# Half-head products for a second batch and an earlier 144 KB load, in a kernel whose instruction order is fixed by a scheduler

## The chip, the cores and the metric

The kernel runs on one core of a Trainium2 chip. The metric is device time in microseconds (us). "Clock" is the mean TensorE clock granted in an execution, 1.0 being full speed. Ratios are the mean time of one kernel's fast runs over the mean of the other's fast runs of the same rounds, so they are not quite the ratio of the medians quoted beside them. Square brackets after a ratio hold its 95% interval. Core engines: TensorE (PE; its weight loads are PEld), VectorE (DVE), ScalarE (ACT), GpSimd (POOL), and SyncE (SP), which issues the loads.

## The reference

Linear attention, then a ResMLP block, for 8 batches, 8 heads, 576 positions, 64 columns per head, in fp32:

```python
kv  = np.einsum('bhsd,bhse->bhde', k, v)
out = np.einsum('bhsd,bhde->bhse', q, kv)
rms = np.sqrt(np.mean(out * out, axis=-1, keepdims=True) + 1e-06)
x   = out / rms * g_norm                       # then heads side by side: (8, 576, 512)
a1  = alpha1 * x + beta1
u   = x + lam * np.einsum('ts,bsd->btd', w_tok, a1)
a2  = alpha2 * u + beta2
y   = u + lam * (np.maximum(a2 @ w_ch1, 0.0) @ w_ch2)     # 512 -> 2048 -> 512
```

The weights are shared by all batches. Until some 48 us the core's DMA engines are nearly always busy with q, k, v and the weights (in the kernel before a mean share of 0.95 from 0 to 48 us, at 341 GB/s); after that TensorE is the bound (busy 312.23 of the 316 us from 48 to 364).

## The kernel before

The Python program records every operation with an engine, a cost estimate in us, its reads and its writes. A list scheduler then fixes the order of each engine **at build time**, from those estimates. At run time an engine works through its list and waits where data is missing, even if the next entry is ready: in the trace of the kernel before, TensorE stands still for 1.14 us, to 41.38 us, for `wst4`, with k'v of batch 1 behind it in the list, whose v had landed at 31.96 us.

q·kv of the first two batches (`R32 = 2`) is done in fp32r. A chunk pair is 256 positions; the fifth chunk (the tail) has 64:

```python
def f32(e):
    if nc_ > 1:                                  # a pair of chunks
        for h in range(nh):
            w = qtr[:, h0 + h, 2 * cs[0]:2 * cs[0] + 2, :].rearrange("p k s -> p (k s)")
            for x in range(1 if nh < 8 else 2):  # 8 heads: two matmuls of N=64 per head
                y = slice(0, 128) if nh < 8 else slice(64 * x, 64 * x + 64)
                # ... o: where the result goes
                mm = e.matmul(o, w, kvr[:, h0 + h, y], start=True, stop=True)
    else:                                        # the tail: 128 rows, 64 of them zeros
        for h in range(h0, hs.stop):
            p = 64 * (h // 4)
            mm = e.matmul(t.flat()[:, 64 * (h - h0):64 * (h - h0) + 64],
                          qtrt[:, h % 4, :], kvr[:, h, p:p + 64], start=True, stop=True)
    return mm
if b < R32:
    P.op("PE", 0.058 * m, f32, cold=True, # ... its reads and writes
```

```python
for hs in (HALVES if b == 0 else ALL):           # batch 0 by half the heads, batch 1 all at once
    for cs in ((0, 2), (1, 3), (4,)):
        yield lambda cs=cs, hs=hs: group(cs, hs)
```

The order of the loads, and the load of the last 64 rows of w_tok into `wst4` ("t2"). "w0" to "w3" are the slices of w_ch1, "w4" and later those of w_ch2, "Bk", "Bv", "Bq" are k, v and q of batch 1:

```python
order = ["k0", "v0", "q0", "k1", "t0", "v1", "q1", "t1",
         "w0", "g", "w1", "w2", "Bk", "Bv", "w3", "Bq", "lam", "a2", "t2", "w4",
         "w5", "w6", "w7"]
# ...
P.op("SP", 0.6, lambda e: e.dma_start(wst4[:], moe_w_tok[8:576:9, :]),
     w=[("wst", 4)], dma_us=0.9, at=sp["t2"])
```

## Time and profile before

| | kernel before |
|---|---|
| device time, median of 3 runs | 365.87 us (364.91 to 366.12) |
| span of the profiled execution, clock | 364.2 us, 0.993 |
| TensorE busy | 357.3 us, 98% |
| TensorE idle for `wst4` at 41.38 us | 1.14 us |
| start of the first channel product (L954) | 32.23 us |
| k'v of batch 1 (L602), at half clock | 3.18 us for 140 matmuls |
| channel product 1 of batch 0 done | 59.89 us |
| start of the last addition | 360.28 us |

The last rows are milestones of TensorE's list, read from the chain that ended last. The lines themselves are in the prediction below.

### The profile page before, as it was taken

How to read it: one execution, taken by the hardware profiler on the slowest of the kernel's cores; microseconds unless marked ns; L12 is line 12 of the kernel's file. 1: busy time of each engine (PE TensorE's matmuls, PEld its weight loads, DVE VectorE, ACT ScalarE, POOL GpSimd, SP SyncE). 2: the span in 40 equal slices, each digit the busy share in tenths (PEclk: the TensorE clock that was granted, in tenths of full speed). 3: DMA queues.
4: the chain of work that ended last, by engine and by line, in shares of the span. 5: the costliest groups of instructions: out<-in, count | busy, mean ns of one | idle time of the engine just before them, and what ended most of it. 6: DMA issues, size and time to landing. Idle time of an engine off the chain costs nothing.

```text
span 364.2 us, 8018 instructions
## 1 busy us (share of the span) xinstructions
PE 357.3 (98%) x3594; PEld 215.2 (59%) x3354; DVE 211.4 (58%) x310; ACT 143.7 (39%) x252; POOL 116.2 (32%) x93
## 2 busy tenths in 40 slices
PE   8999899999999999999999999999999999999995
PEld 6888685466754554457654554457754554457644
DVE  3557699872686189823885189724884288620021
ACT  2675057127750158107730157007730156007500
POOL 4377185910064005700281015800751005300000
PEclk9999899999999999999999999999999999999999
DMA  7999996028865677667816684586836510340023
GB/s 286 355 384 363 323 350 250 0 49 113 237 249 117 115 202 283 104 125 170 314 32 127 117 277 174 108 123 142 337 66 124 117 29 2 72 96 21 2 58 86
DMA packets 67558, 59.17 MB, mean 162 GB/s; under 512 B 45552, under 2 KB 45828, under 8 KB 67524
## 3 DMA queue, kind: packets, MB, share of 16 engines
q1 hardware_dynamic: 67472, 58.66, 58.4%
q8 instruction: 27, 0.44, 0.5%
q14 instruction: 7, 0.06, 0.0%
q10 hardware_dynamic: 52, 0.01, 0.0%
HBM read 38.60 MB, written 9.44 MB: 132 GB/s over the span
## 4 chain that ended last, share of the span: by engine, by line
PE 91%; DMA 5%; SPq 2%; ACT 1%; issue 0%; DVE 0%
PE ps L988 34%; PE ps L938 19%; PE ps L923 13%; PE ps L787 8%; PE ps L602 5%; DMA wst<-in_moe_w_tok_dram 3%; DMA vf<-in_v_dram 3%; PE ps L397 2%; PE ps L682 2%; PE ps L1146 2%; PE ps L800 1%; PE ps L695 1%; PE ps L570 1%; SPq L506 1%; PE ps L1189 0%; SPq L1106 0%
## 5 line engine op out<-in xcount | busy, mean ns | idle before, releaser
L988 PE MATMUL ps<-w,ht 128*128 128x512 bf16 (+1 forms) x592 | 129.0, 373 | 0.0
L988 PEld LDWEIGHTS ps<-w,ht 128*128 128x128 bf16 x592 | 56.8, 98 | 64.1 <-issue 1.6
L912 ACT ACTIVATE ht<-ps,bias 128x640 bf16<-128x640 f32 (+2 forms) x98 | 72.5, 742 | 46.4 <-PE ps L938 38.7
L938 PE MATMUL ps<-a2t,w 128*128 128x320 bf16 x512 | 71.9, 299 | 0.0
L762 POOL TENSOR_TENSOR xm<-xm,g_bc 128x1024 f32<-128x1024 f32 (+1 forms) x16 | 33.4, 2085 | 114.9 <-DVE rt L759 112.4
L938 PEld LDWEIGHTS ps<-a2t,w 128*128 128x128 bf16 x512 | 49.5, 98 | 20.3 <-DVE xm L755 0.3
L923 PE MATMUL ps<-a2t,w 128*128 128x512 bf16 x240 | 54.6, 379 | 0.0
L999 DVE TENSOR_TENSOR xm<-ps,xm 128x512 f32<-128x512 f32 (+1 forms) x33 | 22.1, 673 | 53.4 <-PE ps L988 53.4
L633 ACT ACTIVATE kvd<-ps 64x256 bf16<-64x256 f32 x24 | 9.1, 378 | 99.8 <-PE ps L602 99.6
L733 DVE TENSOR_REDUCE small<-sq 128x16 f32<-128x1024 f32 (+3 forms) x27 | 24.8, 928 | 22.9 <-ACT sq L731 22.7
L923 PEld LDWEIGHTS ps<-a2t,w 128*128 128x128 bf16 x240 | 22.7, 98 | 25.1
L787 PE MATMUL ps<-rt,wt 128*128 128x512 bf16 x140 | 31.4, 379 | 0.0
L913 DVE TENSOR_SCALAR ht<-ps,bias 128x512 bf16<-128x512 f32 (+2 forms) x34 | 24.8, 738 | 10.3 <-PE ps L923 4.7
L534 POOL TENSOR_TENSOR qs<-qf,qs 128x512 bf16<-128x512 f32 x14 | 18.5, 1319 | 25.8 <-ACT qs L493 24.8
L731 ACT ACTIVATE sq<-ps 128x1024 f32<-128x1024 f32 (+3 forms) x27 | 21.3, 799 | 12.9 <-PE ps L397 8.2
L771 DVE TENSOR_TENSOR xm<-ps,xm 128x512 f32<-128x512 f32 x28 | 19.1, 688 | 8.9 <-PE ps L787 8.6
L787 PEld LDWEIGHTS ps<-rt,wt 128*128 128x128 bf16 x140 | 13.7, 98 | 16.5
L999 DVE TENSOR_TENSOR xtl<-ps,xtl 128x512 f32<-128x512 f32 x4 | 2.8, 692 | 35.5 <-PE ps L988 35.5
L602 PEld LDWEIGHTS ps<-vf,kf 64*64 64x64 f32 x1152 | 18.9, 140 | 3.5 <-issue 2.5
L602 PE MATMUL ps<-vf,kf 64*64 64x64 f32 x1152 | 20.1, 227 | 0.4 <-DMA vf<-in_v_dram 0.2
L755 DVE TENSOR_TENSOR xm<-ps,small 128x1024 f32<-128x1024 f32 (+1 forms) x18 | 19.7, 1100 | 0.2
L759 POOL TENSOR_TENSOR rt<-xm,e_bc 128x512 bf16<-128x512 f32 (+1 forms) x6 | 9.8, 1635 | 28.4 <-DVE xm L755 27.4
(105 smaller groups left out, 349.5 us busy)
## 6 DMA issues: line engine op xcount, KB each, us to landing
stg<-in_moe_w_ch_dram SPq DMA_DIRECT2D x8, 1024.0 KB, 12.5
kf<-in_k_dram SPq DMA_DIRECT2D x7, 1152.0 KB, 6.6
vf<-in_v_dram SPq DMA_DIRECT2D x7, 1152.0 KB, 8.7
qf<-in_q_dram SPq DMA_DIRECT2D x7, 1152.0 KB, 10.2
out_dram<-xm SPq DMA_DIRECT2D x62, 128.0 KB, 2.4
kf<-in_k_dram SPq DMA_DIRECT2D x2, 576.0 KB, 5.7
vf<-in_v_dram SPq DMA_DIRECT2D x2, 576.0 KB, 9.4
qf<-in_q_dram SPq DMA_DIRECT2D x2, 576.0 KB, 8.3
```

Of the source, the lines that this page charges most:

```text
L602: m = e.matmul(t.ap(slice(64 * i, 64 * i + 64))[:, y, 64 * x_:64 * x_ + 64], kf[rows, x, c], vf[rows, x, c], start=(c == 0), stop=(c == 8) ...
L731: P.op("ACT", act_us(64 * m), lambda e: e.activation(both(sqv), raw(), ACT.Square), r=[t], w=[("sq", sqs)])
L733: P.op("DVE", dve_us(64 * m), lambda e: e.tensor_reduce(out=smv, in_=sqv, axis=AX.X, op=ALU.add), r=[("sq", sqs)], w=[("sm", sms)], pri=-20)
L755: P.op("DVE", dve_us(64 * m), lambda e: e.tensor_tensor(out=x3, in0=raw(), in1=inv(), op=ALU.mult), r=[t, ("sm", sms)], w=xk, pri=-200)
L762: P.op(dve_pool(64 * m) if b < 2 else "POOL", pool_us(64 * m), lambda e: e.tensor_tensor(out=x3, in0=x3, in1=gb, op=ALU.mult), r=xk + ["g" ...
L787: m = e.matmul(t.flat(), wt[:, sc if sc < 4 else 4 + b % 2, 128 * c:128 * c + 128], rt[:, rs(b, sc), :], start=(sc == 0), stop=(sc == 4))
L912: return e.activation(dst, src(), ACT.Relu, bias=bi)
L913: return e.tensor_scalar(out=dst, in0=src(), scalar1=bi, scalar2=0.0, op0=ALU.add, op1=ALU.max)
L923: m = e.matmul(t.flat(), w1[:, dj, 128 * fj:128 * fj + 128], a2t[:, dj, 0:512], start=(dj == 0), stop=(dj == 3))
L938: m = e.matmul(t.ap()[:, i, 0:320], w1[:, dj, 128 * fj:128 * fj + 128], a2t[:, dj, 320 * i:320 * i + 320], start=(dj == 0), stop=(dj == 3))
L988: m = e.matmul(t.flat()[:, 0:m_], ht[:, fj, 128 * c:128 * c + 128], w2[:, fj, lo:hi], start=(fj == 0), stop=(fj == 15))
L999: P.op("DVE", dve_us(m_), lambda e: e.tensor_tensor(out=x, in0=t.flat()[:, 0:m_], in1=x, op=ALU.add), r=[t] + keys, w=keys)
```

## The change

Its intent: give batch 1 the cheaper form of q·kv that batch 0 already has, and bring in the last w_tok rows before they are needed.

```diff
-                            for x in range(1 if nh < 8 else 2):
-                                y = slice(0, 128) if nh < 8 else slice(64 * x, 64 * x + 64)
-                                o = (t.flat().rearrange("p (c h d) -> p c h d", c=2, d=64)[
-                                    :, :, h, :] if nh < 8 else t.cols(64 * (nh * x + h), 64))
-                                mm = e.matmul(o, w, kvr[:, h0 + h, y], start=True, stop=True)
+                            o = t.flat().rearrange("p (c h d) -> p c h d", c=2, d=64)
+                            mm = e.matmul(o[:, :, h, :], w, kvr[:, h0 + h, :],
+                                          start=True, stop=True)
                     else:
                         for h in range(h0, hs.stop):
-                            p = 64 * (h // 4)
+                            r_ = slice(64 * (h // 4), 64 * (h // 4) + 64)
                             mm = e.matmul(t.flat()[:, 64 * (h - h0):64 * (h - h0) + 64],
-                                          qtrt[:, h % 4, :], kvr[:, h, p:p + 64],
+                                          qtrt[r_, h % 4, :], kvr[r_, h, r_],
...
-                    P.op("PE", 0.058 * m, f32, cold=True,
+                    P.op("PE", 0.1 + (0.06 if nc_ > 1 else 0.12) * m, f32, cold=True,
...
-            for hs in (HALVES if b == 0 else ALL):
+            for hs in (HALVES if b < R32 else ALL):
...
-                 "w0", "g", "w1", "w2", "Bk", "Bv", "w3", "Bq", "lam", "a2", "t2", "w4",
+                 "w0", "g", "w1", "w2", "Bk", "Bv", "t2", "w3", "Bq", "lam", "a2", "w4",
...
-             w=[("wst", 4)], dma_us=0.9, at=sp["t2"])
+             w=[("wst", 4)], slack=4.0, dma_us=0.9, at=sp["t2"])
```

The tail's 64 rows belong to the halves: with 128 rows and halves in batch 1, the race analysis finds that half 0's tail reads rows which half 1's copy still writes. Lines after the cuts shift by two or three (L695 is L692 in the changed kernel, L699 is L697, L1146 is L1144, L923 is L921, L988 is L986, L954 is L952).

## The prediction

> **What bounds the kernel now.** I read the page first, then the chain that ended last in order of time, then one-microsecond windows around the only gap, then the groups of the lines that the change touches. The page's busy times come first, to see which engine could be the bound:
>
> ```profile
> PE 357.3 (98%) x3594; PEld 215.2 (59%) x3354; DVE 211.4 (58%) x310; ACT 143.7 (39%) x252; POOL 116.2 (32%) x93
> PE 91%; DMA 5%; SPq 2%; ACT 1%; issue 0%; DVE 0%
> ```
>
> The first line is busy time: TensorE 98%, everything else under 60%. The second is the chain by engine: TensorE carries 91% of the span. So a microsecond of TensorE work counts in full, if it lies where the chain runs over TensorE. That has to be looked up in the chain in order of time (start, length, what):
>
> ```profile
> 31.09 10.16 DMA wst<-in_moe_w_tok_dram
> 41.25 0.14 issue
> 41.38 1.24 PE ps L1146 x16
> ...
> 42.82 3.13 PE ps L602 x138
> ...
> 50.38 3.49 PE ps L695 x32
> ...
> 54.75 0.81 PE ps L699 x8
> ...
> 360.28 0.42 DVE xm L999
> ```
>
> From 41.38 to 360.26 us every piece is TensorE. Ahead of it stands a transfer: the last 64 rows of w_tok (the tile wst4, "wst" in the profile), issued at 31.09 us as the last of five and landed at 41.25 us. TensorE's timeline shows the gap that it makes:
>
> ```profile
> 39.30 0.94 PE L1215 MATMUL ps<-b2hl,w 128*128 128x2 bf16 x32
> 41.38 1.24 PE L1146 MATMUL ps<-ident,wst 64*64 64x64 f32 x16 [1.14 <-DMA wst<-in_moe_w_tok_dram]
> ```
>
> TensorE stands still for 1.14 us, though other work (the k'v of batch 1, slices 2 and 3 of the first channel product) had its data; the order is fixed at build time and has the transposes first. The windows show a second price. Columns after the times are busy PE, PEld, DVE, ACT and POOL, then granted clock, DMA share and GB/s:
>
> ```profile
> 40.00:41.00 1.00, 0.24 (x10) 0.15 (x7) 0.45 (x3) 0.00 (x0) 0.00 (x0) 1.00 1.02 252
> 41.00:42.00 1.00, 0.62 (x10) 0.65 (x12) 0.00 (x0) 0.00 (x0) 0.00 (x0) 0.79 1.10 401
> 42.00:43.00 1.00, 1.00 (x32) 1.00 (x33) 0.14 (x1) 0.34 (x1) 0.00 (x0) 0.50 1.00 371
> 43.00:44.00 1.00, 1.00 (x50) 1.00 (x47) 0.61 (x3) 0.04 (x1) 0.27 (x1) 0.50 1.04 381
> 44.00:45.00 1.00, 1.00 (x49) 1.00 (x45) 1.00 (x2) 0.00 (x0) 1.00 (x1) 0.51 1.04 385
> ```
>
> Right after the gap the granted clock is 0.50 for over 3 us. The whole change therefore acts between some 28 and 56 us, and its effect is read there.
>
> [...] the trace's fp32r q.kv with 64 moving columns runs at 3.49/32 = 109 ns each[...]. [...] w_ch1's last slice, q of batch 1, lam and alpha2 were issued before wst4, and it landed 10.16 us after its issue though it has 144 KB. [...] Here a square of 128x512 takes 597 ns and one of 128x1024 1024 ns, so a split costs 170 ns.
>
> **The change part by part.**
>
> (1) q.kv of batch 1 by head halves. Removed: 32 matmuls with 64 moving columns, 3.49 us in the chain. Added: 16 with 128 columns, one weight load per head and chunk pair in place of two. Batch 0 already does it so: in the same chain "17.64 1.04 PE ps L695 x8", 0.130 us each. 16 x 0.130 = 2.08 us; saved 3.49 - 2.08 = **1.41 us**, all on the path.
>
> (2) The tail chunk (both fp32r batches) contracts over the 64 rows that hold data instead of 128 zero-padded ones. Same count, same 128 weight columns[...]. Now 8 take 0.81 us together and 4 alone 0.56 us; in batch 1 eight become two groups of four, which may cost up to 2 x 0.56 - 0.81 = 0.31 us. I take **+0.1 us**.
>
> (3) Vector work of batch 1, whose six groups replace three. VectorE: reduce 4 x 0.681 - 2 x 1.213 = +0.30, normalise 4 x 0.690 - 2 x 1.224 = +0.31, tails 2 x 0.406 - 0.684 and 2 x 0.416 - 0.695 = +0.27, reciprocals 4 x 0.168 + 2 x 0.165 - 2 x 0.241 - 0.199 = +0.32: 1.2 us. ScalarE: squares 4 x 0.597 - 2 x 1.024 = +0.34, tail 2 x 0.377 - 0.592 = +0.16, three more square roots at 0.29 = +0.88: 1.4 us. It lies beside TensorE work. VectorE is busy 15.26 of 16.20 us from 48 to 64.2, so this is not free for it; but the finer groups start earlier, and the next thing that needs them has room: batch 1's last rt product ends at 62.66 and its token product starts at 64.21; its last transposed chunk is copied at 78.5 and the channel product that reads it starts at 82.81. I count **0**, with a risk below.
>
> (4) wst4 issued before w_ch1's last slice, whose issue waits for a buffer until 28.32 us. It can then go out right after v of batch 1, at about 18.3 us, 13 us earlier. The queue moves some 380 GB/s in these windows, so 144 KB delay what follows by 0.4 us: w_ch1's last slice lands near 35.1 instead of 34.7, while its channel products run after 47 us. From lam and alpha2 on the sum of bytes is the same. wst4 should land before 30 us, over 9 us ahead of need. Saved: the gap, **1.14 us**.
>
> (5) With the gap gone the clock should stay up. Price of the slow window: k'v of batch 1, 3.18 us for 140 matmuls, against 2.26 us for 144 in every later batch (15.7 ns each, 2.20 us): 0.98. Transposes: 16 in 1.24 us (78 ns) against 64 in 4.37 us (68 ns) for the earlier rows: 0.15. Together **1.1 us**.
>
> (6) slack=4.0 and the new cost estimates only alter the order that the list scheduler fixes. They add no operations; they shuffle the order from about 10 us on. I take **+0.3 us** for it.
>
> Sum if all comes off: 1.41 - 0.1 + 1.14 + 1.1 - 0.3 = 3.25 us. Weighing the clock part at 0.85 leaves 3.1 us: 365.87 - 3.1 = **362.8 us**, 0.8% less.
>
> **The rivals.** (a) The gap moves: TensorE runs into another transfer. DMA engines are above 0.8 share nearly everywhere to 48 us, and TensorE will be some 2 us early at k'v. For it: q of batch 1 and the w_ch2 slices land late (w_ch2's first at 43.7). Against it: [...] w_ch2 is first needed at 59.7. A new wait would give back up to 1 us: near 364. (b) The clock still drops[...]. Against it: from 16.4 to 22 us TensorE runs fp32 transposes almost alone at clock 1.00, and k'v of batch 2 at full rate. [...] That makes 363.9. (c) VectorE and GpSimd become the bound between 50 and 83 us: three w_ch2 products run on GpSimd only at 65.12 to 69.95 and are needed at about 76.8, and TensorE arrives 3 us earlier, with up to 2 us of added vector work. Slack of about 5 us speaks against a stall, but it shrinks. If it bites, 1 to 2 us are lost: 364 to 365. (d) Better than the sum: the new order also removes filler matmuls before 32 us. There TensorE follows the loads, so I expect little: 361.5 at best.
>
> **Range and chances.** The floor of the change is part (1) alone, about 364.5; all parts with a lucky order give 361.3. I take 361.3 to 364.8. A gain over 2% would need 7.3 us, more than twice all parts; a loss over 2% would need a new stall of 10 us in a stretch that has slack. So 0.02 faster, 0.97 same, 0.01 slower.
>
> **What the changed profile would show.** (1) q.kv in batch 1 as 16 matmuls 128x128 at about 0.130 us. (2) Tail matmuls on 64 rows, 0.10 to 0.14 us apart. (4) wst4 issued near 18 us, no TensorE gap on it, its transposes anywhere from 32 us on. (5) Clock 1.00 throughout 32 to 56 us and k'v of batch 1 in about 2.3 us. (3) No TensorE idle between 50 and 83 us. Wrong would be: a TensorE gap with another releaser, a clock of 0.5 in another window, or the start of the first channel product (32.23 us now) moved by more than 0.5 us.

The sum came to 1.41 - 0.1 + 1.14 + 1.1 - 0.3 = 3.25 us, or 3.1 with the clock part at 0.85. Three steps are estimates: that the clock stays up once the gap is gone, for which the trace shows only that half clock began at 41.57 us, 0.19 us after the gap ended; that the tails cost 0.1 us, within the 0 to 0.31 us named; and, in rival (a), that q of batch 1 arrives in time.

## The result, and the profile after

| kernel, set of runs | median us (lowest to highest) | ratio to the kernel before |
|---|---|---|
| changed, first set, 4 executions | 363.75 (363.61 to 364.51) | 0.9956 [0.9932, 0.998] |
| changed again, second set, 5 | 363.37 (363.17 to 363.76) | 0.9928 [0.9914, 0.9941] |
| changed again, third set, 5 | 363.12 (363.0 to 363.56) | 0.9935 [0.992, 0.9951] |
| before, in the same three sets, 4 / 11 / 11 | 365.51 / 366.02 / 365.75 | |

The gain is 0.4% to 0.7%, so within 2%. The first time lies 0.95 us above the predicted 362.8 and inside the range. That could pass for a confirmation; the trace says otherwise. First the page of the changed kernel: busy times, and the chain by engine.

```profile
PE 353.6 (98%) x3543; PEld 213.6 (59%) x3335; DVE 207.1 (57%) x321; ACT 147.5 (41%) x262; POOL 113.1 (31%) x93
PE 93%; DMA 3%; DVE 1%; SPq 1%; issue 1%
```

TensorE's share is unchanged. In the chain DMA fell from 5% to 3%, which is the `wst4` load that left it. The chain in order of time (start, length, what), the changed kernel:

```profile
34.03 3.51 PE ps L952 x32
...
41.37 1.12 PE ps L1144 x16
...
43.20 2.26 PE ps L602 x144
...
55.07 3.40 PE ps L921 x15
58.47 7.34 PE ps L986 x34
...
358.60 0.42 DVE xm L997
```

TensorE's timeline (start, length with the modelled tail, what; a wait in brackets):

```profile
41.30 1.19 PE L1144 MATMUL ps<-ident,wst 64*64 64x64 f32 x16
...
43.13 2.33 PE L602 MATMUL ps<-vf,kf 64*64 64x64 f32 x144
...
49.53 1.19 PE L692 MATMUL ps<-kvr,qtr 128*128 128x128 f32 x8
50.65 0.63 PE L697 MATMUL ps<-kvr,qtrt 64*128 64x64 f32 x4
...
55.07 3.40 PE L921 MATMUL ps<-a2t,w 128*128 128x512 bf16 x15 [0.46 <-DVE small L737]
```

The transposes have no bracket any more: the wait for `wst4` is gone. Yet they begin at 41.37 us, where they began at 41.38 before. TensorE no longer waits there; it is late. The reason stands at the top of the chain: the first channel product starts at 34.03 us instead of 32.23. The windows show where that was lost, and that the clock did stay up where the prediction looked (columns: window, length, busy PE, PEld, DVE, ACT, POOL, then clock, DMA share, GB/s):

```profile
14.00:15.00 1.00, 1.00 (x59) 1.00 (x48) 0.69 (x2) 0.19 (x1) 0.23 (x1) 0.60 1.04 385
15.00:16.00 1.00, 1.00 (x16) 0.82 (x9) 0.65 (x3) 0.27 (x1) 1.00 (x1) 0.50 1.04 385
16.00:17.00 1.00, 1.00 (x7) 1.00 (x6) 0.97 (x3) 0.31 (x1) 0.27 (x2) 0.50 1.05 384
17.00:18.00 1.00, 1.00 (x8) 0.68 (x8) 0.15 (x1) 0.96 (x3) 1.00 (x1) 0.69 0.49 162
```

```profile
42.00:43.00 1.00, 1.00 (x25) 0.93 (x23) 0.22 (x1) 0.38 (x1) 0.00 (x0) 1.00 1.00 375
43.00:44.00 1.00, 1.00 (x66) 0.98 (x65) 0.77 (x3) 0.21 (x1) 0.00 (x0) 1.00 1.05 383
```

At 42 to 44 us the clock is 1.00, and 66 matmuls fit into a microsecond that took 50 before. But half clock has moved to 14 to 17.5 us, in the middle of batch 0's work. In the kernel before, the clock was full there; its line for 13 to 19 us:

```profile
13.00:19.00 6.00, 5.85 (x118) 4.93 (x119) 3.83 (x12) 3.88 (x10) 3.27 (x3) 1.00 0.88 321
```

**The ledger.** From the first channel product to the end of batch 0's first channel stage the changed kernel takes 58.47 - 34.03 = 24.44 us, the kernel before 59.89 - 32.23 = 27.66 us: 3.22 us less. Its terms, from the two traces: gap 1.14; k'v 3.18 - 2.26 = 0.92; transposes 1.24 - 1.12 = 0.12; q·kv of batch 1, 3.49 - 2 x 0.84 = 1.81; its tails 0.81 - 2 x 0.56 = -0.31; a new wait for VectorE, -0.46. Sum 3.22; smaller differences, of up to 0.14 us, cancel. The times of one kind of matmul are taken from the end of the one before to its own last end. The prediction for this stretch was 1.41 - 0.1 + 1.14 + 1.1 = 3.55. Ahead of the stretch 1.80 us are lost, after it 0.26 are gained (not followed further): 3.22 - 1.80 + 0.26 = 1.68 = 360.28 - 358.60. So the stretch that was predicted came out nearly as predicted, and half of its gain was paid elsewhere.

### The profile page after: what moved, and what is told of

Its sections match the earlier page's. It is cut to its first block, busy times and chain, and to the rows that moved or that the text cites. A ratio compares the mean times of both kernels' runs of the same rounds, so it can differ in the third digit from the quotient of the medians.

```text
span 362.2 us, 7967 instructions
## 1 busy us (share of the span) xinstructions
PE 353.6 (98%) x3543; PEld 213.6 (59%) x3335; DVE 207.1 (57%) x321; ACT 147.5 (41%) x262; POOL 113.1 (31%) x93
## 4 chain that ended last, share of the span: by engine, by line
PE 93%; DMA 3%; DVE 1%; SPq 1%; issue 1%
PE ps L986 34%; PE ps L936 19%; PE ps L921 14%; PE ps L785 8%; PE ps L602 5%; DMA vf<-in_v_dram 3%; PE ps L397 2%; PE ps L682 2%; PE ps L1144 2%; PE ps L798 1%; PE ps L819 1%; PE ps L570 1%; PE ps L952 1%; DVE w L1268 1%; SPq L506 1%
## 5 line engine op out<-in xcount | busy, mean ns | idle before, releaser
L986 PE MATMUL ps<-w,ht 128*128 128x512 bf16 (+1 forms) x569 | 125.8, 373 | 1.8 <-issue 1.0
L986 PEld LDWEIGHTS ps<-w,ht 128*128 128x128 bf16 x592 | 56.8, 98 | 64.0 <-issue 1.2
L910 ACT ACTIVATE ht<-ps,bias 128x640 bf16<-128x640 f32 (+2 forms) x100 | 74.1, 744 | 45.8 <-PE ps L936 37.9
L760 POOL TENSOR_TENSOR xm<-xm,g_bc 128x1024 f32<-128x1024 f32 (+1 forms) x17 | 35.0, 2061 | 111.4 <-DVE rt L757 109.3
L921 PE MATMUL ps<-a2t,w 128*128 128x512 bf16 x231 | 53.3, 380 | 0.9 <-DVE small L737 0.5
L921 PEld LDWEIGHTS ps<-a2t,w 128*128 128x128 bf16 x240 | 22.6, 98 | 25.7 <-DVE xm L753 0.7
L911 DVE TENSOR_SCALAR ht<-ps,bias 128x512 bf16<-128x512 f32 (+2 forms) x32 | 22.9, 725 | 11.4 <-PE ps L921 5.1
L771 POOL TENSOR_TENSOR a2b<-xm,a_bc 128x512 bf16<-128x512 f32 x11 | 17.7, 1610 | 17.6 <-DVE xm L769 17.6
L534 POOL TENSOR_TENSOR qs<-qf,qs 128x512 bf16<-128x512 f32 x12 | 15.2, 1266 | 25.5 <-ACT qs L493 24.5
L602 PEld LDWEIGHTS ps<-vf,kf 64*64 64x64 f32 x1152 | 18.0, 137 | 3.5 <-issue 2.5
L602 PE MATMUL ps<-vf,kf 64*64 64x64 f32 x1152 | 19.3, 223 | 0.3 <-DMA vf<-in_v_dram 0.2
```

Source lines behind the costliest of these rows:

```text
L602: m = e.matmul(t.ap(slice(64 * i, 64 * i + 64))[:, y, 64 * x_:64 * x_ + 64], kf[rows, x, c], vf[rows, x, c], start=(c == 0), stop=(c == 8) ...
L760: P.op(dve_pool(64 * m) if b < 2 else "POOL", pool_us(64 * m), lambda e: e.tensor_tensor(out=x3, in0=x3, in1=gb, op=ALU.mult), r=xk + ["g" ...
L910: return e.activation(dst, src(), ACT.Relu, bias=bi)
L911: return e.tensor_scalar(out=dst, in0=src(), scalar1=bi, scalar2=0.0, op0=ALU.add, op1=ALU.max)
L921: m = e.matmul(t.flat(), w1[:, dj, 128 * fj:128 * fj + 128], a2t[:, dj, 0:512], start=(dj == 0), stop=(dj == 3))
L986: m = e.matmul(t.flat()[:, 0:m_], ht[:, fj, 128 * c:128 * c + 128], w2[:, fj, lo:hi], start=(fj == 0), stop=(fj == 15))
```

## The experiments

Questions: is the early half clock caused by the new order or by chance; what is each part worth by itself; and what takes the place of the wait on `wst4`? All runs have correct results and at least five rounds. The expectations name theories by letters or words. The ones that count below: that the order which the new estimates give batch 0 causes the early half clock and keeps the gain down (A, later C); against it, that the half clock falls by chance; and, from the second set on, that TensorE runs out of its own instructions in k'v when it comes there early (F, G).

| run | median us (lowest to highest) | ratio to before of the same set |
|---|---|---|
| a0 changed again | 363.37 (363.17 to 363.76) | 0.9928 [0.9914, 0.9941] |
| a1 load order alone | 369.3 (365.44 to 371.48) | 1.0058 [1.0021, 1.0094] |
| a2 changed, old load order | 364.19 (362.87 to 364.82) | 0.9948 [0.9932, 0.9964] |
| a3 changed, old estimates | 365.53 (364.45 to 367.01) | 0.9994 [0.9972, 1.0016] |
| b1 a1 with k'v later | 369.22 (364.84 to 369.73) | 1.0058 [1.0013, 1.0103] |
| b2 before, `wst4` just after w_ch1's last slice | 364.61 (364.38 to 368.46) | 0.9987 [0.9941, 1.0033] |
| b3 changed, k'v later | 366.74 (365.61 to 367.18) | 1.0009 [0.9975, 1.0042] |
| b4 changed, `wst4` just after the slice | 363.3 (362.27 to 363.65) | 0.9917 [0.9887, 0.9947] |
| c1 changed, old estimates in batch 0 only | 365.01 (362.75 to 365.88) | 0.9977 [0.995, 1.0004] |
| c2 c1 with the old load order | 365.25 (363.57 to 367.12) | 0.999 [0.9962, 1.0018] |
| c3 c1 with b2's load order | 363.33 (363.06 to 364.44) | 0.9946 [0.9928, 0.9965] |
| c4 changed, a third time | 363.12 (363.0 to 363.56) | 0.9935 [0.992, 0.9951] |

The first letter is the set: all runs of a set ran on one chip and share the runs of the kernel before. Two of a1's six executions were slow (371.23 and 371.48 us); its ratio leaves them out.

### a0 and c4: the same kernel again (no edit)

> The changed kernel once more, for the spread. Theory A (the new cost estimates reorder batch 0's first 13 us so that the granted clock falls to half at about 14 us): the profile again has a first channel product near 34.0 us, a clock of 0.5 for about 3.4 us between 14 and 18 us, mean clock 0.995 in most executions, time 363.6 to 364.5. Theory B (the early clock drop is chance, from a late q transfer[...]): the drop is missing in about half the executions, with mean clock 0.999 and times near 362.3 there.

> The changed kernel a third time, beside the three above on the same chip: 363.2 to 363.9, early half clock in most executions (mean clock 0.995), and no more than 0.6 us between executions with it and without it.

a0's profile shows the early half clock again; c4's doesn't. Its first window, then its TensorE timeline:

```profile
14.00:15.00 1.00, 1.00 (x55) 0.75 (x47) 0.26 (x2) 0.18 (x1) 0.84 (x1) 1.00 1.05 391
```

```profile
32.36 3.65 PE L952 MATMUL ps<-a2t,w 128*128 128x256 bf16 x32
...
37.61 2.77 PE L921 MATMUL ps<-a2t,w 128*128 128x512 bf16 x12 [0.73 <-ACT ht L910]
...
40.69 1.20 PE L1144 MATMUL ps<-ident,wst 64*64 64x64 f32 x16
```

So the early half clock isn't in every execution of the changed kernel. Without it the first channel product starts at 32.50 us in the chain, 1.53 earlier. But the last addition starts at 357.76 us, only 0.84 before the 358.60 of the first profile, because TensorE now waits 0.73 us at 37.61 us for a relu copy on ScalarE. ScalarE's own lines tell why: it waited for w_ch1's last slice, which it has to convert first. The line of the kernel before, then that of c4:

```profile
34.68 1.15 ACT L493 ACTIVATE w<-stg 128x512 bf16<-128x512 f32 x2 [2.40 <-DMA stg<-in_moe_w_ch_dram]
```

```profile
36.05 1.15 ACT L493 ACTIVATE w<-stg 128x512 bf16<-128x512 f32 x2 [3.63 <-DMA stg<-in_moe_w_ch_dram]
```

The slice lands 1.4 us later, although it was issued at 27.64 us and not at 28.32, and the relu copy stands behind its conversion in ScalarE's list. Removing one wait made TensorE early enough to meet another.

Over executions, the clock separates two groups. Of the changed kernel's 14 executions, eight have a clock of 0.995 or less, mean 363.69 us, and six 0.998 or more, mean 363.22: 0.47 us apart. Of 32 executions of the kernel before, run beside the experiments (one of 369.41 us at 0.986 left out), 19 have 0.993 or 0.994, mean 366.19, and 13 have 0.998 or more, mean 365.35: 0.84 apart. Half clock is thus no rarer after the change (8 of 14 against 19 of 32). Between the undisturbed groups the gain is 365.35 - 363.22 = 2.13 us. (Only the profiled executions show where their half clock lies; for the others it is taken from the mean.)

### a2: the changed kernel with the old load order

```diff
-                 "w0", "g", "w1", "w2", "Bk", "Bv", "t2", "w3", "Bq", "lam", "a2", "w4",
+                 "w0", "g", "w1", "w2", "Bk", "Bv", "w3", "Bq", "lam", "a2", "t2", "w4",
...
-             w=[("wst", 4)], slack=4.0, dma_us=0.9, at=sp["t2"])
+             w=[("wst", 4)], dma_us=0.9, at=sp["t2"])
```

> Head halves, 64-row tails and cost estimates, with wst4 still issued last; TensorE's whole order is the same as in the changed kernel. Theory A: early clock drop as in the changed kernel, first channel product near 34 us; the gap on wst4 shrinks because TensorE arrives 1.8 us later, so that the time is 0.5 to 1.5 us over the changed kernel, 364.2 to 365.3. Theory B: the early drop comes and goes, and the gap costs its full 1 us plus the slow clock after it, 1 to 2.2 us over the changed kernel.

TensorE's order is that of the changed kernel, so this is a clean comparison of the load order. Its timeline has the old gap, and half clock in k'v after it:

```profile
40.84 1.20 PE L1144 MATMUL ps<-ident,wst 64*64 64x64 f32 x16 [1.14 <-DMA wst<-in_moe_w_tok_dram]
...
42.68 3.49 PE L602 MATMUL ps<-vf,kf 64*64 64x64 f32 x144
```

The ratio is 0.9948 against 0.9928 for a0 of the same set: the load order is worth about 0.0020 x 366 = 0.7 us here (the two intervals overlap a little). The prediction gave 1.14 for the gap and 1.1 for the clock. By their mean clock, five of a2's six executions have half clock somewhere. The sixth, at clock 1.0, took 362.87 us, less than any of the changed kernel's 14. So where the clock stays up, no worth of the new load order is to be seen, the 1.14 us of the gap included; but that is a single execution without a profile.

### a1: the load order alone, in the kernel before

The edit is the reverse of a2's, made in the kernel before. TensorE's order is as before but for 16 of the two-column bias matmuls, which move behind the transposes.

> Only the transfer order of wst4 (with its slack) is changed; the first 39 us of TensorE order are those of the kernel before. Theory A: no gap at 41 us, no early clock drop, first channel product near 32.2 us, 2.2 us less than before, about 363.3. Theory B: the early clock drop shows here as often as in the changed kernel, 363.3 to 364.8. If the predicted price of the gap and of its slow clock is wrong: less than 1 us gained.

It was **slower** than the kernel before, 1.0058. TensorE's timeline:

```profile
38.17 1.90 PE L923 MATMUL ps<-a2t,w 128*128 128x512 bf16 x8 [0.39 <-ACT ht L912]
...
40.38 1.20 PE L1146 MATMUL ps<-ident,wst 64*64 64x64 f32 x16
...
42.22 1.50 PE L602 MATMUL ps<-vf,kf 64*64 64x64 f32 x84
45.75 1.29 PE L602 MATMUL ps<-vf,kf 64*64 64x64 f32 x60 [2.03 <-issue]
```

The gap on `wst4` is gone and the transposes start a microsecond earlier. Then k'v stops after 84 of 144 matmuls for 2.03 us, with no semaphore, engine or data transfer named as releaser ("issue"). Half clock follows:

```profile
47.00:48.00 1.00, 1.00 (x10) 0.85 (x9) 0.84 (x2) 0.79 (x3) 0.92 (x2) 0.50 0.44 147
```

The trace's DMA records hold a candidate: a queue of the kind "instruction" moves 27 packets of 16,384 bytes in an execution. Which engine they serve is not named; that it is TensorE is inferred from the counts: the changed kernel has 3,543 + 3,335 instructions on TensorE, and no other engine has more than 321. That makes about 255 to a packet, an estimate (the profile's page doesn't count every kind). How one of these packets lies to k'v in each run (us, put together from the DMA records and TensorE's timeline):

```
run   packet in flight   k'v starts   stops   resumes   wait   resumes after packet's end
a1    43.35-44.47        42.29        43.72   45.75     2.03   1.28
a3    42.54-43.63        41.57        43.00   45.01     2.02   1.38
c1    42.53-43.66        41.50        42.93   44.96     2.03   1.30
a0    42.24-43.34        43.11        44.55   44.73     0.18   1.39
b2    40.98-42.02        42.05        --      43.55     short  1.53
c4    41.41-42.46        42.60        --      43.98     short  1.51
```

In these four profiles with a stop, TensorE resumes 1.28 to 1.39 us after that packet has landed. The stop comes after 84 matmuls of k'v in a1, a3 and c1 and after 87 in a0, a fixed place in each program, as it would be if one packet's instructions ended there. The starts of single matmuls show short pauses at the same places in b2 and c2 (0.28 us from the 84th start to the 85th) and in c4 (0.16 us from the 87th to the 88th), again 1.30 to 1.53 us after the packet's landing; in the first profile of the changed kernel and in b3, b4 and c3 the packet had landed earlier relative to k'v, and there is no pause. b3 stops later, in batch 2's k'v, and resumes 1.41 us after another such packet. k'v runs through its instructions fast: 144 matmuls and 144 weight loads in 2.26 us, 7.8 ns each, so that 255 of them would last 2.0 us, at a time when the data queues fill the DMA engines (a DMA share of 1.00 to 1.09 in each microsecond from 40 to 45 in the changed kernel). That the late packet, itself 1.0 to 1.1 us in flight, is what TensorE waits for is inferred from these times and from the missing releaser; no run held back or advanced the packet by itself.

The second cost of a1 is in w_ch1's last slice. In the six microseconds after 28 us, the kernel before and then a1:

```profile
28.00:34.00 6.00, 6.00 (x81) 5.49 (x79) 4.58 (x13) 3.03 (x7) 5.22 (x8) 1.00 0.99 361
```

```profile
28.00:34.00 6.00, 6.00 (x82) 5.56 (x79) 4.58 (x13) 3.10 (x7) 5.28 (x8) 1.00 1.02 301
```

The DMA engines are as busy but move 301 GB/s instead of 361, and ScalarE can start on the slice at 36.61 us instead of 34.68, 1.9 us later where 144 KB at 380 GB/s would be 0.4. Why the rate falls is open.

### a3: the changed kernel with the old estimates

```diff
-                    P.op("PE", 0.1 + (0.06 if nc_ > 1 else 0.12) * m, f32, cold=True,
+                    P.op("PE", 0.058 * m, f32, cold=True,
```

> The changed kernel with the old cost estimate in the list scheduler; operations are the same, batch 0's order is that of the kernel before (the first w_tok transposes ahead of v's second half, as there). Theory A: no early clock drop, first channel product near 32.3 us, time near 362.2, 1.5 us better than the changed kernel. Theory B: same as the changed kernel within 0.4 us.

The theory that the new estimates cost the late start expected 362.2 us. The run gave 365.53: all of the gain is gone when only the numbers that steer the scheduler go back. The early half clock was indeed absent in its profile. In its place stand the stop of 2.02 us in k'v, half clock after it, and 0.83 us of waiting for VectorE before the token product at 66.52 us. So the estimates are no cost of the change; with the old ones its gain isn't there.

### b1 and b3: k'v of batch 1 later

The same edit in a1 and in the changed kernel, to let the packet arrive first:

```diff
-                P.op("PE", 0.2 + 1.06 * np_, f, cold=True, w=[t, ("kvp", hs.start)],
+                P.op("PE", 0.2 + 1.06 * np_, f, cold=True, pri=40.0 if b == 1 else 0.0, w=[t, ("kvp", hs.start)],
```

> The transfer order alone (run a1), and k'v of batch 1 put behind the q transposes and four wide matmuls. Theory F (the gain went into a new wait: 144 small k'v matmuls run through their 288 instructions faster than the instruction stream comes, 2.03 us idle in a1, and the clock halves after it): the wait inside k'v falls below 0.5 us, no half clock after it, time 363.3 to 364.8 with a spread under 1.5 us, against 365.4 to 371.5. Theory W (the gain went into the later landing of w_ch1's last slice, which holds the bias-and-relu copies on ScalarE and with them PSUM): no better than a1 by more than 0.7 us.

> The changed kernel with k'v of batch 1 later, as in b1. Theory F: no instruction wait; 0 to 1 us better than the changed kernel, 362.4 to 363.4, the more so in executions without the early clock drop. Theory W: the same as the changed kernel within 0.3 us.

In b1 the stop in batch 1's k'v is gone, as the instruction theory said; the time didn't improve (369.22 us), which it had not said. The copies of kv that q·kv needs now stand later in VectorE's list, behind scalings of w_ch2, and TensorE waits for them:

```profile
49.85 3.73 PE L695 MATMUL ps<-kvr,qtr 128*128 128x64 f32 x32 [0.58 <-DVE kvr L494]
```

Half clock comes in b1 as well, and for longer (0.50 from 54.05 to 60.88 us), though TensorE was busy throughout the 3.41 us before it; the runs don't show why. In b3 it is 0.52 us of such waits, and a stop of 1.07 us in batch 2's k'v. Both runs moved too much at once to price the instruction stop; they show that moving k'v is no remedy.

### b2 and b4: `wst4` just after w_ch1's last slice

b2 is the kernel before, b4 the changed one, each with this order:

```diff
+                 "w0", "g", "w1", "w2", "Bk", "Bv", "w3", "t2", "Bq", "lam", "a2", "w4",
```

> The kernel before with wst4 issued between w_ch1's last slice and q of batch 1; TensorE's order is that of a1. Theory W: the slice lands near 34.7 us as before, no wait of TensorE for the relu copies near 38 us, wst4 lands near 38 us, no gap: 363.0 to 364.0. Theory F: TensorE gets to k'v at 41 to 42 us and stands 1.5 to 2.5 us in it for instructions, the clock halves: 365 to 368.

> The changed kernel with wst4 issued just after w_ch1's last slice; TensorE's order is unchanged. Theory F: the slice lands 0.5 to 1 us earlier and nothing comes of it, 363.0 to 363.8. Theory W: 0.7 us or more better than the changed kernel, 362.6 or less.

TensorE's order in b2 is that of a1. Its timeline:

```profile
40.15 1.19 PE L1146 MATMUL ps<-ident,wst 64*64 64x64 f32 x16
...
41.98 2.71 PE L602 MATMUL ps<-vf,kf 64*64 64x64 f32 x144
```

No gap on `wst4`, only the short pause of the table in k'v, and the clock stays at 1.0 there. Four of b2's six executions took 364.4 to 364.7 us against a median of 366.01 for the kernel before; two took 368.0 and 368.5 at a clock of 0.991, and these two make the ratio 0.9987. So this load order alone can gain 1.4 us, or 1.0 against the four executions of the kernel before that are at 0.998 or more in this set (mean 365.52); whether it does depends on the execution. b4 (0.9917) has the best ratio of all, but the changed kernel's own three sets, 0.9928 to 0.9956, are not clearly worse. I wouldn't call it a better version on this evidence.

### c1, c2, c3: the parts without batch 0's new order

c1 keeps the old estimate for batch 0 only, so batch 0 runs in its old order and batch 1 as in the changed kernel:

```diff
-                    P.op("PE", 0.1 + (0.06 if nc_ > 1 else 0.12) * m, f32, cold=True,
+                    P.op("PE", 0.1 + (0.06 if nc_ > 1 else 0.12) * m if b else 0.058 * m, f32, cold=True,
```

c2 is c1 with the old load order, so in effect parts (1) and (2) alone. c3 is c1 with b2's load order.

> The changed kernel with the old cost estimate for batch 0 alone: batch 0 in the order of before, batch 1 in that of the changed kernel, transfers as in the changed kernel. Theory G (an early TensorE only meets the next waits: relu copies behind the late slice near 38 us, instructions inside k'v near 43 us): no early half clock, first channel product near 32.2 us, over 1 us of instruction wait in k'v and a half clock after it, 363.5 to 366. Theory C (the early half clock of the changed kernel costs its full 1.5 us): 361.7 to 362.4.

> Part (1) with (2) alone: head halves in the order of the kernel before, transfers as before. If the q.kv matmuls are worth what the chain says (32 at 0.109 against 16 at 0.105, less 0.31 for the tails): gap and half clock at 41 us as before, 1.5 us under before, 364.3 to 364.8. If the doubled vector work or PSUM takes it back: less than 0.8 us.

> The order of c1 with wst4 issued after w_ch1's last slice, that is run b2 with head halves. If parts add up: 1.5 us under b2's good executions (364.4 to 364.7), 362.8 to 363.3, instruction packet near 41 us and no wait in k'v, some executions 3 to 4 us slower with a clock of 0.991. Theory W would have it better than the changed kernel by 1 us or more in all executions.

c1 tells theories C and G apart. Its profile has no early half clock and its first channel product starts at 32.18 us, so by C it should win. Its chain:

```profile
41.50 1.43 PE ps L602 x84
42.93 2.03 issue
44.96 1.15 PE ps L602 x60
```

k'v starts 1.1 us earlier than in c4 (42.60), which has no early half clock either, and 1.7 earlier than in the first profile (43.20). It loses 2.03 us there, as G expected; half clock follows from 47 to 50 us. Against c4, the changed kernel in the same set, the ratio is 0.9977 against 0.9935: batch 0's new order is worth about 0.0042 x 366 = 1.5 us, on average. It is worth that by avoiding the disturbance, as far as the clocks show: five of c1's six executions are at 0.995 or less, and the sixth, at 0.998, took 362.75 us, less than any of c4's.

c2 was to show q·kv by halves at 1.5 us and showed a gain of 0.1% [-0.2%, +0.4%]. Sorted by clock it shows more: four executions at 0.994 or 0.995 have a mean of 365.18 us where five of the kernel before (0.993 or 0.994) have 366.26, and the one at 0.999 took 363.57 where six (0.999 or more) have 365.18. That is 1.1 and 1.6 us less; the sixth execution, of 367.12 us at 0.991, takes it back from the mean. Its profile has the early half clock, with batch 0 in its **old** order, and a wait that the halves bring with them:

```profile
52.79 1.04 PE L921 MATMUL ps<-a2t,w 128*128 128x512 bf16 x4 [0.73 <-DVE ht L911]
```

TensorE waits for a relu copy which VectorE does at 51.98 us, behind a scaling of w_ch2 at 50.70. c3's profile has 0.46 us of the same kind. c3 (0.9946) is ahead of c1 and c2 (the intervals overlap a little), so the load order of b2 seems to help batch 0's old order; c3 is level with the changed kernel.

**The early half clock.** It is in four of six profiles with batch 0's new order (the first one, a0, b3, b4) and in two of eight with the old (c2, c3). The same kernel shows it or not. The clock records in the traces narrow it down. Every stretch of half clock before the end lasts 3.41 us (in b1 twice that), and starts a whole number of 3.41 us after the clock first became full, as on a grid: in the kernel before at 41.57 = 4.02 + 11 x 3.413 us, in the first profile of the changed kernel at 14.21 = 3.97 + 3 x 3.413 us. In the six profiles with the early half clock the grid has a point at 13.65 to 14.64 us, and the half clock starts there. Of the other eight, only the kernel before has a point in that range (14.26 us); the seven others have theirs at 11.92 to 13.10 and again at 15.33 to 16.51 us. So where the grid lies in an execution decides much of it, and to that extent it falls by chance, as theory B had it. Among the seven profiles with a point in that range, all four with the new order have the early half clock and two of the three with the old; whether the order adds anything stays open. Nor do the traces show what brings a half clock on. None of the stretches of 3.41 us before a half clock that were looked at was idle throughout: TensorE had a matmul in flight for 2.27 us in the kernel before (with the gap of 1.14), 1.38 in a1 (with the stop of 2.03), 3.21 in the first profile of the changed kernel, and for all of it in b1.

## Why the prediction was right and where it was wrong

The time was in its range, and the verdict (within 2%) was the one given 0.97. Point by point:

- **(1) q·kv by halves**: right in mechanism. 16 matmuls took 1.68 us, 0.105 us each and not batch 0's 0.130, so 1.81 us were saved on TensorE, not 1.41. The 0.130 was a misreading: it spreads what the change from and to other work costs over eight matmuls, whose starts, past the first, are 0.112 us apart in batch 0 as in batch 1. The starts are 0.112 us apart with N=64 too. Alone in batch 0's old order (c2) it gained nothing clear in the mean, and 1.1 to 1.6 us by clock, from few executions.
- **(2) tails**: +0.31 us, the upper limit named, not +0.1.
- **(3) vector work, counted 0**: the first profile has 0.46 us of TensorE waiting for it, a0 and c4 none, c2 and c3 0.73 and 0.46. The size was off: a few tenths, not always there. Rival (c) was there in this small form.
- **(4) the gap**: it went, as said. `wst4` was issued at 18.26 us, as forecast, but landed only 15.1 us later, at 33.4 us and not before 30; that was still early enough. And "144 KB delay what follows by 0.4 us" failed: w_ch1's last slice came 0.6 to 1.9 us later over the runs with the change's load order, which made a new wait for its conversion (0.39 us in a1, 0.73 in c4). In a1 and c4 it was issued at 28.38 and 27.64 us, against 28.32 before; in the first profile and a0, with the early half clock, 0.84 and 0.75 us of the delay are a later issue. The load order's net worth was 0.7 us in the changed kernel (a2), and less than nothing alone (a1).
- **(5) "with the gap gone the clock should stay up"**: this step, an estimate, failed. The clock did stay up at 41 to 46 us, for 0.92 us in k'v and 0.12 in the transposes, against 1.1 predicted. But half clock then appears at 14 to 17.5 us in four of six profiles with batch 0's new order, or after a new stop in a1, a3 and c1. With 8 of 14 executions disturbed against 19 of 32, the clock term gave almost nothing net. It was also too large from the start: half clock costs the kernel before 0.84 us in 19 of 32 executions, so 0.5 us on average. Take the term out of the sum and 1.41 - 0.1 + 1.14 - 0.3 = 2.15 is left, where the undisturbed executions measure 2.13. That is luck: the sum agrees, its terms, as shown, do not. In undisturbed executions the load order shows no gain, neither in a1 (365.44 us, where three of the kernel before have a mean of 365.45) nor against a2 (362.87), while q·kv by halves (c2) shows 1.6 us; each rests on one execution.
- **(6) "+0.3 us" for the estimates**: this step failed in sign. What they do to batch 0 is worth 1.5 us of gain (c1 against c4). In c1's profile, without them, TensorE comes to k'v 1.1 us earlier than in c4's and stops there for 2.03 us.
- **Rival (a)**, a new wait in place of the old, was right in kind. It named late q and w_ch2 transfers; what came was the relu copy behind w_ch1's late slice, and a packet of TensorE's own instructions. The prediction had listed "the start of the first channel product moved by more than 0.5 us" among what would make it wrong; it moved by 1.80 in the first profile.
- **Rival (b)**, the clock still drops, came true, though at 14 us and not where it was looked for. Its 363.9 us counts the 0.85 twice: 3.25 - 1.1 leaves 363.7.

What stays open: why the instruction packet lands as late as 43.3 to 44.5 us in a0, a1, a3, b1, c1 and c2 and at 42.0 to 43.1 elsewhere; whether batch 0's order adds to the early half clock; why w_ch1's last slice comes so late; and the worth of each part, since the parts don't add: in the mean, loads alone made it slower, halves alone changed nothing clear, and the whole is faster.

## What to carry to other kernels

When you remove a wait, ask what the engine meets if it arrives there earlier, and count its own instruction supply among the things that may be late: that is what the stop of 2.03 us in a1 points to, in 288 instructions at 7.8 ns each beside a DMA share of 1.02 to 1.07, though no run tested it alone. In a kernel ordered by a list scheduler an estimate is part of the change: measure it apart from the operations, and measure the parts together as well, because they need not add. Sort executions by granted clock before explaining differences below 1%: here the clock alone separated executions of one kernel by 0.47 and 0.84 us, 0.13% and 0.23%.
